# H3 convolution and MLP on one core: copies shared by ScalarE and VectorE get PSUM tiles of their own, two blocks and one output tile go in halves

## Chip, cores and metric

The kernel runs on 1 core of one Trainium2 chip. The metric is device time in microseconds (us). In this text PE is TensorE, PEld its weight loads, ACT is ScalarE, DVE is VectorE, POOL is GpSimd and SP is SyncE; all times are us unless marked otherwise.

## The reference

One layer of an H3 block on 2048 tokens with 512 channels, in bf16, followed by an MLP with 1376 hidden units. The long convolution is computed there with Fourier transforms of length 4096 over the tokens.

```python
def _A_ref(q, k, v, shift_k, ssm_k, ssm_D):
    ...
    for t in range(ks):                                   # ks = 4
        k_shift = k_shift + k_pad[:, t:t + S, :] * shift_k[:, ks - 1 - t][None, None, :]
    kv = k_shift * v
    L = 2 * S
    ...
    kv_f = rfft2(kv_pad[:, None, :, :], axes=(1, 2))      # over 4096 tokens, half of them zero
    kf_f = rfft2(kf_pad[:, None, :], axes=(1, 2))         # the filter ssm_k
    y_f = kv_f * kf_f
    y = irfft2(y_f, s=(1, L), axes=(1, 2)).astype(bf16)[:, 0, :S, :]
    y = y + kv * ssm_D[None, None, :]
    return q * y

x = A_q
h = x + _A_ref(_layernorm(x), A_k, A_v, A_shift_k, A_ssm_k, A_ssm_D)
h2 = h + relu(_layernorm(h) @ B_w1) @ B_w2
return h2
```

## The kernel before

The Fourier transforms are matmuls in two stages each way. The order of instructions on every engine is the order of the source (a manual schedule); the framework places the semaphore waits and gives out buffers.

- **PSUM.** Until inverse stage 1 is over, every PSUM tile comes from one pool, `psF`, of four buffers of two banks each (`bank2`: 128 x 2 x 512 floats). A new tile takes the buffer that the fourth tile before it had, and its first writer waits until that tile's readers are done.
- **Transposition, `to_rows` (lines 271 to 284).** It runs twice: for the filter `sk` (line 311, into `kfl`) and for the product `vT` (line 387, into `xfl`). PE transposes 32 pieces in four groups h = 0 to 3 of eight (line 276). A group fills one PSUM tile `pst` and is copied out into every 32nd column range of the destination: h = 0 and 2 by ACT (line 281), h = 1 by DVE (line 283), and h = 3 by both, four pieces each.
- **Stage 1 (`stage1`, lines 286 to 309).** Sixteen pairs of matmuls (line 294) fill two PSUM tiles. For the filter the two tiles are each read by both engines (DVE line 306, ACT line 309); for the product ACT reads one and DVE the other (lines 267 and 269 through `copy`). Between the filter's groups PE computes the four taps of the short convolution (`taps`, line 333), whose result DVE multiplies with v (line 337). ACT computes sines for the tables of later stages in between.
- **Stage 2 and product (lines 418 to 455).** PE at lines 425 and 435, ACT at 415, DVE at 442, and POOL builds tables at 380.
- **Inverse stage 1 (`inv1`, lines 550 to 562).** Sixteen blocks b. A block has four groups i of three matmuls (line 541) into one PSUM tile `psi`; then one engine copies it out in two pieces, into the two halves of `ax` (one of them lies in the tile `BX`). Blocks 6, 8, 10, 12 and 14 are copied by DVE, block 15 by both engines, two groups each, the others by ACT. Behind the copies of blocks 8 to 11 ACT computes a sine table each (line 262), DVE computes layer norm statistics behind block 0 and normalises behind block 3, and SP loads x behind block 11.
- **Inverse stage 2 and MLP (lines 626 to 712).** For each of four quarters q: `inv2` (line 634), `gate` (DVE, lines 620 and 621), `mlp1` (PE line 646, ReLU on ACT line 648) and `mlp2`. In `mlp2` an output tile of 128 tokens x 512 channels is 11 matmuls (line 659), one DVE pass that scales and adds the residual (line 662), and one store on ACT's queue (line 665). The output buffers `ob` are three, used in turn.

The first matmul of inverse stage 2 needs all 128 columns of `ax`, so it needs the copies of all sixteen blocks. The first of stage 1 needs the whole of `kfl` or `xfl`.

Of the kernel before, what the change touches and what calls it, by code (L numbers as in the profile page):

```python
# [9 lines left out]
ALU = mybir.AluOpType  # L10
BF16 = mybir.dt.bfloat16
F32 = mybir.dt.float32
F32R = mybir.dt.float32r
I32 = mybir.dt.int32
PSUM = bass.MemoryType.PSUM
P = 128
# [40 lines left out]
def kernel(  # L57
# [13 lines left out]
    nc = tc.nc  # L71
    _, S, D = A_q.shape
    DFF = B_w1.shape[1]
    KS = A_shift_k.shape[1]
    assert S == 2048 and D == 512 and KS == 4, "kernel is specialised to S=2048, D=512, ks=4"
    NT = 16
    DC = D // P
    NFC = (DFF + P - 1) // P
    x_d, k_d, v_d, out_d = A_q[0], A_k[0], A_v[0], out[0]
# [70 lines left out]
    def bank2(name):  # L150
        return psum.tile([P, 2, 512], F32, tag="ps", name=name)[:]
# [23 lines left out]
    identw = early.tile([P, P], F32, name="identw")  # L175
# [81 lines left out]
    def ec_wrap(q):  # L257
        nc.vector.tensor_single_scalar(out=ecw[q], in_=ecw[q], scalar=8191, op=ALU.bitwise_and)  # L258

    def ec_sins(q, rs=range(DC)):  # L260
        for r in rs:
            nc.scalar.activation(out=ecore[q][:, :, :, r, :], in_=ecw[q].rearrange("p h (i x) -> p h i x", i=4),  # L262
                                 func=ACT.Sin, scale=esc[:, r:r + 1], bias=ebi[:, r:r + 1])

    def copy(eng, o, i):
        if eng == "A":
            nc.scalar.copy(out=o, in_=i)
        else:
            nc.vector.tensor_copy(out=o, in_=i)

    def to_rows(src, h, fl):

        pst = bank2("pst").rearrange("p b (i c) -> p (b i) c", i=4)
        srcw = src.bitcast(F32).rearrange("p c (a w) -> p (c a) w", w=32)
        for i in range(8):
            nc.tensor.transpose(out=pst[:, i, :], in_=srcw[:, :, 8 * h + i], identity=identw[:])
        o = fl.bitcast(I32)
        for eng, i0, n in {0: (("A", 0, 8),), 1: (("D", 0, 8),), 2: (("A", 0, 8),), 3: (("A", 0, 4), ("D", 4, 4))}[h]:
            oi, pi = o[:, :, 8 * h + i0:8 * h + i0 + n], pst[:, i0:i0 + n, :]
            if eng == "A":  # L280
                nc.scalar.copy(out=oi.bitcast(F32), in_=pi.rearrange("p i c -> p c i"))
            else:
                nc.vector.tensor_single_scalar(out=oi, in_=pi.bitcast(I32).rearrange("p i c -> p c i"),
                                               scalar=0, op=ALU.bitwise_or)

    def stage1(fl, B, gb, dmul=None):
# [24 lines left out]
    for h in range(4):  # L311
        to_rows(sk, h, kfl)
# [74 lines left out]
    for h in range(4):  # L387
        to_rows(vT, h, xfl[:])
# [86 lines left out]
    xh = [None] * 4  # L475

    def load_x(q):
        for a, src in enumerate(_tokens(x_d, 4 * q, 4)):
            nc.sync.dma_start(out=xh[q][32 * a:32 * a + 32].rearrange("p t d -> p (t d)"), in_=src)
# [8 lines left out]
    rstd2 = late.tile([P, NT, 1], F32, name="rstd2")  # L488
# [24 lines left out]
    def ln1_stats(q):  # L513
        stats(xh[q], mv1, rstd1, q)

    def ln1_norm(q, src=None):

        src = xh[q] if src is None else src
        for i in range(4):
            t = 4 * q + i  # L520
            nc.vector.tensor_scalar(out=src[:, i, :], in0=src[:, i, :], scalar1=mv1[:, t, 0:1],
                                    scalar2=rstd1[:, t, :], op0=ALU.subtract, op1=ALU.mult)
        rows_T(qT[q], src)

    def center(n):
        fs = slice(n * FS, (n + 1) * FS)
        nc.vector.tensor_tensor(out=w1[:, :, fs], in0=w1[:, :, fs],
                                in1=cen[n].unsqueeze(1).to_broadcast([P, DC, FS]), op=ALU.subtract)
# [3 lines left out]

    blocks = {}

    def inv1_mm(b, i, parts):
        g = 4 * b + i
        o = blocks[b][:, i].rearrange("p d a n -> p (d a n)")
        for part in parts:
            src = BX[:, 0] if part == 0 else BK[:, part - 1]
            rhs = inv3[:].rearrange("p d a n -> p (d a n)") if part == 0 else inv12[:, 4 - 2 * part:8 - 2 * part, :].rearrange("p a n -> p (a n)")  # L540
            nc.tensor.matmul(out=o, lhsT=src[:, g // 2, :, g % 2::2].rearrange("p c r -> p (c r)"), rhs=rhs,  # L541
                             start=(part == 0), stop=(part == 2), skip_group_check=True)

    def inv1_begin(b):

        blocks[b] = bank2("psi").rearrange("p b (i d a n) -> p (b i) d a n", i=2, d=2, a=2)
        for i in (0, 2):
            inv1_mm(b, i, (0,))

    def inv1(b, eng):  # L550
        if b in blocks:
            for i in range(4):
                inv1_mm(b, i, (0, 1, 2) if i % 2 else (1, 2))
        else:
            blocks[b] = bank2("psi").rearrange("p b (i d a n) -> p (b i) d a n", i=2, d=2, a=2)
            for i in range(4):
                inv1_mm(b, i, (0, 1, 2))
        ps = blocks[b]
        for e, i0, n in ((eng, 0, 4),) if len(eng) == 1 else ((eng[0], 0, 2), (eng[1], 2, 2)):
            for rho in range(2):  # L560
                copy(e, ax[rho][:, :, :, 8 * b + 2 * i0:8 * b + 2 * i0 + 2 * n],
                     ps[:, i0:i0 + n].rearrange("p i d a n -> p a n (i d)")[:, rho].rearrange("p (n m) c -> p n m c", m=2))

    lift(0)
    later = qT[0].rearrange("p i r t -> p (i r t)").bitcast(F32)[:, 0:2 * FS].rearrange("p (n f) -> p n f", n=2)
# [6 lines left out]
    ecw[1] = xr1.rearrange("p i d -> p (i d)").bitcast(I32).rearrange("p (h x) -> p h x", h=2)  # L572
    ec_turns(1)
    for b in range(16):
        inv1(b, "AD" if b == 15 else "D" if b in (6, 8, 10, 12, 14) else "A")
        if b == 0:
            for n in range(4):
                center(n)
            ec_wrap(1)
            ln1_stats(0)  # L580
        if b == 3:
            ln1_norm(0)
        if b in (8, 9, 10, 11):
            ec_sins(1, (b - 8,))
        if b == 11:
            load_x(1)
# [4 lines left out]
    def room(n, pat, **kw):  # L591

        top[0] += n
        assert top[0] <= 32768
        return M[:, top[0] - n:top[0]].rearrange(pat, **kw)

    w2 = room(NFC * 512, "p (c d) -> p c d", c=NFC)
# [54 lines left out]
    def mlp2(sc, hook=None):  # L652
        h1T = h1s[sc]
        for i in range(4):
            t = 4 * sc + i
            ps2 = psm.tile([P, D], F32, tag="ps", name="ps2m")
            for fc in range(NFC):
                ksz = min(P, DFF - fc * P)
                nc.tensor.matmul(out=ps2[:], lhsT=h1T[:ksz, fc, i * P:(i + 1) * P], rhs=w2[:ksz, fc, :],  # L659
                                 start=(fc == 0), stop=(fc == NFC - 1))  # L660
            o = ob[t % 3]
            nc.vector.scalar_tensor_tensor(out=o[:], in0=ps2[:], scalar=rstd2[:, t, :], in1=xh[sc][:, i, :],  # L662
                                           op0=ALU.mult, op1=ALU.add)
            dst = bass.AP(tensor=out_d.tensor, offset=out_d.offset + t * D, ap=[[16 * D, 4], [64 * D, 32], [1, D]])
            nc.scalar.dma_start(out=dst, in_=o)
            if hook is not None:
                hook(i)

# [8 lines left out]
    psm = pl.push("psM", bufs=4, space=PSUM)  # L677
# [11 lines left out]
    def next_norm(q):  # L689
# [7 lines left out]
        return hook  # L697

    mlp2(0, next_norm(2))
    inv2(2, psz)  # L700
    mlp1(1, lambda fc: ec_sins(3, (fc // 2,)) if fc in (1, 3, 5, 7) else None)
    stats(xh[1], mv2, rstd2, 1)
    gate(2)
    mlp2(1, next_norm(3))
    inv2(3, psz)
    mlp1(2)
    stats(xh[2], mv2, rstd2, 2)
    gate(3)
    mlp2(2)
    mlp1(3)  # L710
    stats(xh[3], mv2, rstd2, 3)
# [32 lines left out]
```

## Time and profile before

| what | value |
|---|---|
| runs before | 214.94, 214.96, 216.5; median 214.96 |
| the profiled execution's own time | 214.74 |
| its span, first to last instruction | 213.0 |
| mean granted clock of PE | 0.994 |
| first transposition (line 276) | 9.49 to 13.33 |
| taps and stage 1 of the filter | 14.75 to 36.9 |
| second transposition | 36.91 to 40.73 |
| stage 1 of the product | 42.15 to 51.5 |
| stage 2 and product | 51.56 to 91 |
| inverse stage 1 (line 541) | 90.8 to 114.5 |
| inverse stage 2, gate, MLP | 116.11 to 207.75 |
| last store: issue, end of the span | 208.56, 213.0 |

The profile's rows in order of time read: start, duration, engine, line, operation, output<-input, partitions x elements and type, count; in square brackets how long the engine stood idle before, and what ended that idle time. A row for several instructions spans all of them. "Matmul" rows have ends that are modelled, so the distance between starts tells PE's pace better than their length. The profiled time is a little longer than the span, since the span counts from the first to the last instruction.

### The profile page before, as it was taken

The numbers are of one execution on the slowest core, as the hardware profiler recorded it, in microseconds if no ns is written. First come the engines' busy times: TensorE is split into PE (matmuls) and PEld (weight loads), VectorE is DVE, ScalarE is ACT, GpSimd is POOL, SyncE is SP. The second block draws the span as 40 slices with busy tenths as digits, with TensorE's granted clock in tenths as the row PEclk, the third lists the DMA queues.
The fourth block names the chain that finished last, engine by engine and source line by source line (L and its number), as shares of the span: only waits on it lengthen the run. The fifth ranks groups of instructions, "written<-read, shape, count | busy, mean of one in ns | idle before, by whom it ended". The sixth has DMA issues, their size and how long they took to land. (4 is left out here: it accounts for less than half of the span.)

```text
span 213.0 us, 4286 instructions
## 1 busy us (share of the span) xinstructions
PE 200.3 (94%) x1715; PEld 137.1 (64%) x1724; DVE 141.2 (66%) x243; ACT 115.7 (54%) x186; POOL 70.3 (33%) x119
## 2 busy tenths in 40 slices
PE   7779999999999999999997999999999999999990
PEld 2465555887888888789996954457444844444440
DVE  5978987599678887898743487897078742260121
ACT  3987776687777677657592039501970065026200
POOL 7954703995555893030103022420102110002000
PEclk9999999999999999999999999999999999999997
DMA  5999970001600000037315997999818715110011
GB/s 155 340 219 171 197 118 2 3 5 15 252 3 0 3 0 3 0 99 102 67 32 143 267 210 142 174 170 142 110 33 101 141 24 102 27 57 14 0 51 47
DMA packets 47686, 19.91 MB, mean 93 GB/s; under 512 B 42706, under 2 KB 46132, under 8 KB 47668
## 3 DMA queue, kind: packets, MB, share of 16 engines
q1 hardware_dynamic: 44144, 16.15, 41.1%
q10 hardware_dynamic: 3524, 3.51, 5.6%
q8 instruction: 13, 0.21, 0.5%
q14 instruction: 5, 0.04, 0.1%
HBM read 7.02 MB, written 2.10 MB: 43 GB/s over the span
## 5 line engine op out<-in xcount | busy, mean ns | idle before, releaser
L648 ACT ACTIVATE M<-ps1m 128x512 bf16<-128x512 f32 (+1 forms) x44 | 25.0, 601 | 49.9 <-PE ps1m L646 39.5
L659 PE MATMUL ps2m<-M 128*128 128x512 bf16 (+1 forms) x172 | 38.5, 379 | 0.2
L659 PEld LDWEIGHTS <-M 128*128 128x128 bf16 (+1 forms) x176 | 17.1, 98 | 20.9 <-ACT M L648 0.4
L646 PEld LDWEIGHTS <-w 128*128 128x128 bf16 (+1 forms) x176 | 17.4, 100 | 20.4 <-issue 0.7
L380 POOL TENSOR_TENSOR smc<-st 64x256 fp32r<-64x256 f32 x32 | 22.7, 729 | 11.1 <-PE us L435 10.2
L662 DVE SCALAR_TENSOR_TENSOR M<-ps2m,rstd,M 128x512 bf16<-128x512 f32 x12 | 9.0, 748 | 25.3 <-PE ps2m L659 16.8
L503 POOL TENSOR_SCALAR rstd<-mv 128x4 f32<-128x4 f32 x8 | 2.2, 276 | 70.9 <-DVE mv L501 70.9
L541 PE MATMUL psi<-inv,BK 128*128 128x256 f32 x128 | 22.7, 283 | 0.0
L442 DVE TENSOR_TENSOR BK<-u,ktu 128x512 fp32r<-128x512 f32 x32 | 20.4, 680 | 0.0
L541 PEld LDWEIGHTS psi<-inv,BK 128*128 128x128 f32 x128 | 19.9, 195 | 0.0
L646 PE MATMUL ps1m<-xT,w 128*128 128x512 bf16 (+1 forms) x88 | 19.6, 379 | 0.2 <-ACT M L648 0.2
L646 PE MATMUL ps1m<-M,w 128*128 128x512 bf16 (+1 forms) x88 | 19.3, 379 | 0.0
L541 PE MATMUL psi<-inv,BX 128*128 128x256 f32 x64 | 18.0, 286 | 0.1
L415 ACT COPY ktu<-u 128x512 f32<-128x512 f32 x32 | 17.2, 589 | 1.5
L442 DVE TENSOR_TENSOR BX<-us,kts 128x512 fp32r<-128x512 f32 x16 | 11.1, 691 | 8.4 <-PE u L425 6.7
L415 ACT COPY kts<-us 128x512 f32<-128x512 f32 x16 | 9.4, 587 | 9.5 <-PE us L435 9.5
L425 PE MATMUL u<-BK,st 64*128 64x256 f32 x128 | 14.6, 308 | 0.0
L425 PE MATMUL u<-BX,st 64*128 64x256 f32 x128 | 13.0, 284 | 0.0
L309 ACT CAST BK<-ps 128x512 fp32r<-128x512 f32 x16 | 9.4, 585 | 6.5 <-PE ps L294 3.9
L541 PEld LDWEIGHTS psi<-inv,BX 128*128 128x128 f32 x64 | 12.3, 195 | 0.6 <-DVE BK L442 0.6
L499 DVE BATCH_NORM_STATS2 st<-M 128x6 f32<-128x512 bf16 x20 | 12.3, 677 | 0.0
L435 PE MATMUL us<-BK,smc 128*128 128x256 f32 x64 | 12.0, 310 | 0.0
(127 smaller groups left out, 399.3 us busy)
## 6 DMA issues: line engine op xcount, KB each, us to landing
E<-in_A_ssm_k_dram SPq DMA_DIRECT2D x1, 2048.0 KB
out_dram<-M ACTq DMA_DIRECT2D x16, 128.0 KB
w<-in_B_w_dram SPq DMA_DIRECT2D x1, 1376.0 KB
M<-in_B_w_dram ACTq DMA_DIRECT2D x1, 1280.0 KB
M<-in_A_q_dram SPq DMA_DIRECT2D x8, 128.0 KB
xh<-in_A_q_dram SPq DMA_DIRECT2D x4, 128.0 KB
xr<-in_A_q_dram SPq DMA_DIRECT2D x4, 128.0 KB
M<-in_B_w_dram ACTq DMA_DIRECT2D x1, 96.0 KB
```

The costliest lines, as they stand in the source:

```text
L309: nc.scalar.copy(out=o[1 - rp][:, 1], in_=pv[1 - rp][:, 1])
L380: nc.gpsimd.tensor_tensor(out=smc[pq, c % 4, i, :, 64 * dp:64 * dp + 64], in0=st[pq, ks, 64:128].bitcast(F32), in1=st[pq, ks, 0:64].bitcas ...
L415: nc.scalar.copy(out=kt[:], in_=ps)
L425: nc.tensor.matmul(out=ps[:, dp, 256 * x:256 * x + 256], lhsT=t[pq], rhs=cols((BK, BX)[x], pq, k1, i), start=(i == 0), stop=(i == 1), tile ...
L435: nc.tensor.matmul(out=ps[:, k % 2, 256 * x:256 * x + 256], lhsT=smc[:, k // 4 % 4, i, k % 4, :], rhs=cols((BK, BX)[x], slice(0, P), k, i) ...
L442: nc.vector.tensor_tensor(out=o, in0=ps[:, :, 256:512].rearrange("p b (g x) -> p b g x", x=8), in1=kt[:].rearrange("p b (g x) -> p b g x", ...
L499: nc.vector.bn_stats(out=st[:, i, :], in_=src[:, i, :])
L541: nc.tensor.matmul(out=o, lhsT=src[:, g // 2, :, g % 2::2].rearrange("p c r -> p (c r)"), rhs=rhs, start=(part == 0), stop=(part == 2), sk ...
L646: nc.tensor.matmul(out=ps1[:fsz, :].rearrange("p (i t) -> p i t", i=4), lhsT=w1[:, c, fc * P:fc * P + fsz], rhs=hT[sc][:, :, c, :], start= ...
L648: nc.scalar.activation(out=h1T[:fsz, fc, :], in_=ps1[:fsz, :], func=ACT.Relu)
L659: nc.tensor.matmul(out=ps2[:], lhsT=h1T[:ksz, fc, i * P:(i + 1) * P], rhs=w2[:ksz, fc, :], start=(fc == 0), stop=(fc == NFC - 1))
L662: nc.vector.scalar_tensor_tensor(out=o[:], in0=ps2[:], scalar=rstd2[:, t, :], in1=xh[sc][:, i, :], op0=ALU.mult, op1=ALU.add)
```

## The change

- In `to_rows` each copy gets a PSUM tile of its own. For h = 0, 1 and 2 nothing differs. For h = 3 the four transposes of ACT's half go into one tile and the four of DVE's half into another; each tile takes a whole buffer of the pool and uses half of it.
- In `inv1` the same is done for blocks that are shared: two groups into a tile, its copies, then two groups into a second tile, its copies. Blocks 14 and 15 are now shared; blocks 7, 9, 11 and 13 go to DVE (before: 6, 8, 10, 12 and 14), the others to ACT.
- In `mlp2` the last of the 16 output tiles is computed, passed through DVE and stored in two halves of 256 channels: 22 matmuls of 256 columns instead of 11 of 512, two DVE passes, two stores of 128 rows of 512 bytes.

```diff
     def to_rows(src, h, fl):
-        pst = bank2("pst").rearrange("p b (i c) -> p (b i) c", i=4)
...
-        for i in range(8):
-            nc.tensor.transpose(out=pst[:, i, :], in_=srcw[:, :, 8 * h + i], identity=identw[:])
...
+        for eng, i0, n in {1: (("D", 0, 8),), 3: (("A", 0, 4), ("D", 4, 4))}.get(h, (("A", 0, 8),)):
+            pst = bank2("pst").rearrange("p b (i c) -> p (b i) c", i=4)[:, 0:n]
+            for i in range(n):
+                nc.tensor.transpose(out=pst[:, i, :], in_=srcw[:, :, 8 * h + i0 + i], identity=identw[:])
...
     def inv1(b, eng):
...
-        ps = blocks[b]
-        for e, i0, n in ((eng, 0, 4),) if len(eng) == 1 else ((eng[0], 0, 2), (eng[1], 2, 2)):
+        n = 4 // len(eng)
+        for i0, e in zip((0, 2), eng):
+            if b not in blocks or i0:
+                blocks[b] = bank2("psi").rearrange("p b (i d a n) -> p (b i) d a n", i=2, d=2, a=2)
+                todo = [(i, (0, 1, 2)) for i in range(n)]
...
+            for i, parts in todo:
+                inv1_mm(b, i, parts, i0)
             for rho in range(2):
                 copy(e, ax[rho][:, :, :, 8 * b + 2 * i0:8 * b + 2 * i0 + 2 * n],
...
-        inv1(b, "AD" if b == 15 else "D" if b in (6, 8, 10, 12, 14) else "A")
+        inv1(b, "AD" if b > 13 else "D" if b in (7, 9, 11, 13) else "A")
...
             o = ob[t % 3]
-            nc.vector.scalar_tensor_tensor(out=o[:], in0=ps2[:], ...)
-            dst = bass.AP(tensor=out_d.tensor, offset=out_d.offset + t * D, ap=[[16 * D, 4], [64 * D, 32], [1, D]])
-            nc.scalar.dma_start(out=dst, in_=o)
+            w = D // 2 if t == NT - 1 else D
+            for d0 in range(0, D, w):
+                ps2 = psm.tile([P, D], F32, tag="ps", name="ps2m")[:, 0:w]
+                for fc in range(NFC):
+                    ksz = min(P, DFF - fc * P)
+                    nc.tensor.matmul(out=ps2, lhsT=h1T[:ksz, fc, i * P:(i + 1) * P], rhs=w2[:ksz, fc, d0:d0 + w],
+                                     start=(fc == 0), stop=(fc == NFC - 1))
+                nc.vector.scalar_tensor_tensor(out=o[:, d0:d0 + w], in0=ps2, ...)
+                dst = bass.AP(tensor=out_d.tensor, offset=out_d.offset + t * D + d0, ap=[[16 * D, 4], [64 * D, 32], [1, w]])
+                nc.scalar.dma_start(out=dst, in_=o[:, d0:d0 + w])
```

More of the change, by code (lines that the diff above doesn't have):

```diff
@@ L271, in to_rows @@
     def to_rows(src, h, fl):
-        pst = bank2("pst").rearrange("p b (i c) -> p (b i) c", i=4)
         srcw = src.bitcast(F32).rearrange("p c (a w) -> p (c a) w", w=32)
-        for i in range(8):
-            nc.tensor.transpose(out=pst[:, i, :], in_=srcw[:, :, 8 * h + i], identity=identw[:])
         o = fl.bitcast(I32)
-        for eng, i0, n in {0: (("A", 0, 8),), 1: (("D", 0, 8),), 2: (("A", 0, 8),), 3: (("A", 0, 4), ("D", 4, 4))}[h]:
-            oi, pi = o[:, :, 8 * h + i0:8 * h + i0 + n], pst[:, i0:i0 + n, :]
+        for eng, i0, n in {1: (("D", 0, 8),), 3: (("A", 0, 4), ("D", 4, 4))}.get(h, (("A", 0, 8),)):
+            pst = bank2("pst").rearrange("p b (i c) -> p (b i) c", i=4)[:, 0:n]
+            for i in range(n):
+                nc.tensor.transpose(out=pst[:, i, :], in_=srcw[:, :, 8 * h + i0 + i], identity=identw[:])
+            oi = o[:, :, 8 * h + i0:8 * h + i0 + n]
             if eng == "A":
-                nc.scalar.copy(out=oi.bitcast(F32), in_=pi.rearrange("p i c -> p c i"))
+                nc.scalar.copy(out=oi.bitcast(F32), in_=pst.rearrange("p i c -> p c i"))
             else:
-                nc.vector.tensor_single_scalar(out=oi, in_=pi.bitcast(I32).rearrange("p i c -> p c i"),
+                nc.vector.tensor_single_scalar(out=oi, in_=pst.bitcast(I32).rearrange("p i c -> p c i"),
                                                scalar=0, op=ALU.bitwise_or)
@@ L533, with inv1_mm @@
     blocks = {}
-    def inv1_mm(b, i, parts):
-        g = 4 * b + i
+    def inv1_mm(b, i, parts, i0=0):
+        g = 4 * b + i0 + i
         o = blocks[b][:, i].rearrange("p d a n -> p (d a n)")
@@ L550, in inv1 @@
     def inv1(b, eng):
[L551 to L557, printed above, removed]
-        ps = blocks[b]
-        for e, i0, n in ((eng, 0, 4),) if len(eng) == 1 else ((eng[0], 0, 2), (eng[1], 2, 2)):
+        n = 4 // len(eng)
[3 more added lines that the diff above has]
+                todo = [(i, (0, 1, 2)) for i in range(n)]
+            else:
+                todo = [(i, (0, 1, 2) if i % 2 else (1, 2)) for i in range(n)]
+            for i, parts in todo:
+                inv1_mm(b, i, parts, i0)
             for rho in range(2):
                 copy(e, ax[rho][:, :, :, 8 * b + 2 * i0:8 * b + 2 * i0 + 2 * n],
-                     ps[:, i0:i0 + n].rearrange("p i d a n -> p a n (i d)")[:, rho].rearrange("p (n m) c -> p n m c", m=2))
+                     blocks[b][:, 0:n].rearrange("p i d a n -> p a n (i d)")[:, rho].rearrange("p (n m) c -> p n m c", m=2))
     lift(0)
@@ L655, in mlp2 @@
             t = 4 * sc + i
[L656 to L660, printed above, removed]
-            o = ob[t % 3]
-            nc.vector.scalar_tensor_tensor(out=o[:], in0=ps2[:], scalar=rstd2[:, t, :], in1=xh[sc][:, i, :],
-                                           op0=ALU.mult, op1=ALU.add)
-            dst = bass.AP(tensor=out_d.tensor, offset=out_d.offset + t * D, ap=[[16 * D, 4], [64 * D, 32], [1, D]])
-            nc.scalar.dma_start(out=dst, in_=o)
+            o = ob[t % 3]
+            w = D // 2 if t == NT - 1 else D
[5 more added lines that the diff above has]
+                                     start=(fc == 0), stop=(fc == NFC - 1))
+                nc.vector.scalar_tensor_tensor(out=o[:, d0:d0 + w], in0=ps2, scalar=rstd2[:, t, :], in1=xh[sc][:, i, d0:d0 + w],
+                                               op0=ALU.mult, op1=ALU.add)
+                dst = bass.AP(tensor=out_d.tensor, offset=out_d.offset + t * D + d0, ap=[[16 * D, 4], [64 * D, 32], [1, w]])
+                nc.scalar.dma_start(out=dst, in_=o[:, d0:d0 + w])
             if hook is not None:
```

## The prediction

> **What bounds the kernel now.** I read the page's busy times first, then the busy time by stage, then the order of instructions around each edited place, and last what moves after the last matmul. TensorE (PE) is at work for 94% of the span, so a change pays only where PE stands still, or behind PE's last matmul.
>
> ```profile
> PE 200.3 (94%) x1715; PEld 137.1 (64%) x1724; DVE 141.2 (66%) x243; ACT 115.7 (54%) x186; POOL 70.3 (33%) x119
> ```
>
> The edits touch four places. In the first transposition PE waits for the last copy, in the order of time:
>
> ```profile
> 11.57 1.23 DVE L283 TENSOR_SCALAR E<-pst 128x1024 int32<-128x1024 int32 x1 [0.37 <-PE pst L276]
> 12.47 1.50 ACT L281 COPY E<-pst 128x1024 f32<-128x1024 f32 x2 [0.69 <-PE pst L276]
> 14.00 0.69 DVE L283 TENSOR_SCALAR E<-pst 128x512 int32<-128x512 int32 x1 [1.21 <-ACT E L281]
> ...
> 14.75 0.23 PE L294 MATMUL ps<-f_hi,E 64*128 64x128 bf16 x2 [1.42 <-DVE E L283]
> ```
>
> VectorE (DVE) is free from 12.80, the last transpose ends at 9.49 + 3.84 = 13.33, yet DVE starts its half at 14.00, when ScalarE (ACT) has done the other half of the same tile. The same wait of 1.21 stands in the second transposition:
>
> ```profile
> 39.87 1.50 ACT L281 COPY xfl<-pst 128x1024 f32<-128x1024 f32 x2 [0.78 <-PE pst L276]
> ...
> 41.41 0.69 DVE L283 TENSOR_SCALAR xfl<-pst 128x512 int32<-128x512 int32 x1 [1.21 <-ACT xfl L281]
> 41.80 0.59 ACT L309 CAST BK<-ps 128x512 fp32r<-128x512 f32 x1 [0.43 <-PE ps L294]
> 42.01 1.28 DVE L306 TENSOR_TENSOR BK<-ps,dmask 128x512 fp32r<-128x512 f32 x2
> ...
> 43.34 1.23 DVE L269 CAST BX<-ps 128x1024 fp32r<-128x1024 f32 x1
> 43.38 1.01 ACT L267 CAST BX<-ps 128x1024 fp32r<-128x1024 f32 x1
> ```
>
> The last two rows say that it is the shared PSUM tile that makes the wait: there the engines copy from tiles of their own into interleaved columns of one output, and they run side by side. At the end of inverse stage 1 the wait is on the path, for PE stands idle until DVE is done:
>
> ```profile
> 114.52 0.37 ACT L267 CAST BX<-psi 128x256 fp32r<-128x256 f32 x1 [1.80 <-PE psi L541]
> ...
> 114.79 0.38 ACT L267 CAST ax<-psi 128x256 fp32r<-128x256 f32 x1
> ...
> 115.20 0.42 DVE L269 CAST BX<-psi 128x256 fp32r<-128x256 f32 x1 [0.83 <-ACT ax L267]
> ...
> 115.54 0.41 DVE L269 CAST ax<-psi 128x256 fp32r<-128x256 f32 x1
> 116.11 0.36 PE L634 MATMUL pz<-core,BX 128*128 128x256 f32 x1 [1.39 <-DVE ax L269]
> ```
>
> And behind PE's last matmul stand one VectorE pass and one store; the windows (PE, PEld, DVE, ACT, POOL busy, clock, DMA share, GB/s) show bytes until about 211.45, then nothing:
>
> ```profile
> 207.78 0.75 DVE L662 SCALAR_TENSOR_TENSOR M<-ps2m,rstd,M 128x512 bf16<-128x512 f32 x1 [1.63 <-PE ps2m L659]
> ```
> ```profile
> 207.25:209.25 2.00, 0.49 (x3) 0.00 (x0) 0.75 (x1) 0.00 (x0) 0.00 (x0) 1.00 0.22 66
> 209.25:211.50 2.25, 0.00 (x0) 0.00 (x0) 0.00 (x0) 0.00 (x0) 0.00 (x0) 0.74 0.20 58
> 211.50:213.00 1.50, 0.00 (x0) 0.00 (x0) 0.00 (x0) 0.00 (x0) 0.00 (x0) 0.50 0.00 0
> ```
>
> **First transposition: 0.59 us saved.** No instruction is added, only one more of the four PSUM buffers is taken. Its transposes reuse the buffer of h=0, copied by 10.79 + 0.99 = 11.78, while they start at about 12.7 (28 transposes at 0.115, which is 3.84 less the 0.275 of one, over 31): no stall. DVE's start follows the last transpose as 11.57 follows the sixteenth, by 0.08: 13.41, and 0.69 later it ends at 14.10. ACT's half ends at 12.47 + 1.50 = 13.97. PE's stage 1 starts 0.06 behind, at 14.16 and not 14.75. What follows until the second transposition is paced by PE: its stage 1 starts at 20.61, 23.44, 26.28 and 29.12, every 2.83, and DVE in each round waits 0.33 to 0.53 for PE's taps. The loads do not shift, but their SyncE (SP) rows end at 28.64 and DMA is silent from 31.0, while DVE uses the last of them at 33.79. So the whole 0.59 is carried on. DVE's wrap at 14.61 moves to 14.02, behind the GpSimd (POOL) row that feeds it and ends at 13.78. If a load or that POOL row were the hidden bound, the saving would be 0: bounds 0 and 0.65.
>
> **Second transposition: nothing.** DVE's half can start at 40.81 instead of 41.41 (0.08 behind the last transpose at 40.73). But PE works on stage 1 of the last filter group in between (40.66 to 41.73), and does not need this copy. The extra buffer shifts who waits for whom: that stage's second PSUM tile stood four behind h=1 (free at 40.20), and now four behind h=2, whose ACT copy ends at 39.87 + 1.01 = 40.88. PE waits there about 0.22, so L309 and L306 start at about 42.02, against 41.80 and 42.01. DVE's L306 pair, then L269, follow back to back, and DVE sets the pace of the next stage (10.65 of 10.90 busy from 42.1 to 53). It starts where it did. I take 0; bounds: 0.10 lost, 0.21 won if the buffer is free sooner.
>
> **End of inverse stage 1: 0.68 saved.** DVE's half of block 15 waits only for its own matmuls, and they end at 114.09 + 0.40 = 114.49, as ACT's first copy showed at 114.52. DVE's two copies then run from 114.52 to 115.27, as they now run from 115.20 to 115.95, and PE starts inverse stage 2 at 115.43. ACT's half is ready at about 113.8 and done at 114.5. Block 14 in halves is done on DVE at 113.85. PE keeps its 192 matmuls, at 0.12 each, and hardly waited there (23.41 busy of 23.5).
>
> The engines of blocks 6 to 14 are swapped by one. ACT now has blocks 8, 10 and 12 with the four sines between them: 104.47 + 0.94 (pair of copies) + 2 x 1.14 (sines) + 0.94 + 2.28 gives 110.91, and block 12 is done at 111.95. Behind ACT's sines waits SP's load of x (now at 111.41): it goes 0.4 earlier. POOL's tables and the load of w2 on ACT's queue wait for PE's last matmul, which stays. DVE's block 13 is done at 112.94. Block 15's two tiles need the buffers of blocks 12 and 13 at 113.05 and 113.77: 1.1 and 0.8 to spare, and that spare is what hides this edit. Late next, after 115.43, is PE's own inverse stage 2, then the gate, the statistics and ACT's sines down to 132.8; the chain that ended last runs through them, all started by it, and PE is dense behind. Bounds 0.55 and 0.70.
>
> **Last output tile: 0.65 saved.** PE gets 22 matmuls of 256 columns for 11 of 512. The nearest rows are L634's, 256 columns with a weight load each, at 0.117 apart: 22 x 0.117 = 2.57 against 11 x 0.216 = 2.38, so 0.19 lost (bounds 0 and 0.27, by L541's 0.12). VectorE's pass shrinks as its 256- and 512-wide casts do, 0.42 to 0.69: 0.75 to 0.46, 0.29 won. The group starts at 205.37; the halves end on PE at 206.66 and 207.94, on DVE at 207.15 and 208.43, and the stores are issued at 207.18 and 208.46 (0.55 each on ACT's queue, with nothing else behind). The store alone thus starts 0.10 sooner. Bytes begin 1.05 behind an issue (208.56 to 209.6). The store before moves bytes from 207.25 to 209.1, at 0.28 of the DMA engines, so the first half queues behind it. A 128 KB store takes 1.75, 1.33 at the 98 GB/s of its later part. A half takes 0.67 if bytes count, 1.35 if its 128 rows count as they do at 1 KB; I take 0.85, nearer to the bytes, for the rate is steady. The second half's bytes could begin at 209.51 but find the first's until 209.95, which hides both PE's 0.19 and VectorE's 0.29; without that cover they are a net gain of 0.10. Halves end at 209.95 and 210.80, against 211.45: 0.65 saved; with rows alone 211.80, 0.35 lost; with bytes alone 210.5, 0.95 saved. What follows the bytes (1.55) stays. The first half's pass needs its output buffer back from the fourth store from the end, bytes until 204.5 and 1.55 more: 206.05, and it starts at 206.69, so no wait is added there.
>
> A rule speaks against this edit: the Trainium skill, "DMA: Bandwidth & Descriptors", section Bandwidth, calls transfers under 64 KB dominated by descriptors, and lists 0.95 us for 64 KB. By it the halves would end at 211.0 and the whole saving would be 0.2 smaller. No row here has a transfer of 64 KB in such rows.
>
> **The sum.** 0.59 + 0 + 0.68 + 0.65 = 1.92. The profiled execution took 214.74 around its span of 213.0, so it would take 212.82; the median of the runs is 0.22 higher, 213.04. I forecast 213.0.
>
> **Rivals.** (a) Rows and not bytes set the halves' store: 0.59 + 0.68 - 0.35 = 0.92 saved, 214.0. For it: the share of 0.28 says few engines carry a store. Against: the steady 98 GB/s. (b) The early saving is swallowed before inverse stage 1, because a load or POOL sets the start of a later step: 1.33 saved, 213.6. Against: PE is the releaser in every round. (c) The upper ends: the second transposition wins 0.21, the stores 0.95: 2.43 saved, 212.5. (d) The copies still wait on each other, because their outputs interleave: only the stores gain, 214.3. Against: the rows at 43.34 and 43.38. (e) The slower side: ACT's copies of block 12 come so late, behind four sines and blocks 8 and 10, that block 15's first tile finds no free buffer. It decides when they end after 113.05, and the kernel gets slower when they end 1.92 later still, after 114.97; if each of the four sines cost one more of its 1.14, they would end at 116.5, 3.46 late, and the time would be 216.5. Against: the 111.95 above.
>
> **How the numbers follow.** Forecast 0.48, (a) 0.13, (b) 0.09, (c) 0.22, (d) 0.05, (e) 0.03. About 1% is what a measurement of this kernel can tell from no change, here 2.15 saved, below 212.81. The forecast's own range is 212.6 to 213.5, and some 0.11 of its 0.48 lies below that line; with (c) that gives 0.33 for faster. Slower by over 1% is (e), 0.03. The rest, 0.64, is within 1%. The range 212.2 to 214.1 takes in (a), (b) and (c) and leaves out (d), (e) and the far ends.
>
> **What would show it.** Right: no wait of DVE L283 for ACT; stage 1 at about 14.16; the step from L276's last transpose to L269's first copy in the second transposition unchanged, with PE waiting about 0.2 inside it; PE's gap ahead of L634 about 0.7 and not 1.4; no wait of PE for ACT or DVE between blocks 12 and 15; bytes ending some 3 us behind PE's last matmul, against 3.7 now. Wrong: the start of stage 1 earlier but the start of inverse stage 1 not; or the last half's bytes taking over 1.2.

## The result and the profile after

| | before | after |
|---|---|---|
| median of the runs | 214.95 (4 runs) | 212.98 (4 runs) |
| profiled execution: own time, span | 214.74, 212.96 | 213.07, 211.25 |
| mean granted clock of PE | 0.994 | 1.000 |

By the medians 1.97 us are saved, by the two profiled spans 1.71; the ratio of the mean times is 0.9893, with a 95% interval of 0.9852 to 0.9933. Single executions of several of the kernels took some 1.5 more at a lower mean clock (two later ones of the kernel before: 216.35 and 216.41 at 0.986); the last section shows one from inside. In the listing after, lines below `to_rows` have moved: the transposes stand at 278, the matmuls of `mlp2` at 662, its DVE pass at 664.

The page of the changed kernel, part 1, answers to the first line shown of before:

```profile
PE 201.9 (96%) x1735; PEld 138.5 (66%) x1735; DVE 141.4 (67%) x244; ACT 116.1 (55%) x188; POOL 70.4 (33%) x119
```

PE's share went up because the span shrank around nearly the same work; that its busy time reads 1.6 more is mostly a gap in the record of before, which has 1715 matmuls for 1724 weight loads. The timeline of the first transposition after:

```profile
11.64 1.23 DVE L283 TENSOR_SCALAR E<-pst 128x1024 int32<-128x1024 int32 x1 [0.41 <-PE pst L278]
...
12.92 0.52 PEld L278 LDWEIGHTS pst<-identw,E 128*128 128x128 f32 x4 [0.16 <-DVE E L283]
13.67 0.69 DVE L283 TENSOR_SCALAR E<-pst 128x512 int32<-128x512 int32 x1 [0.81 <-PE pst L278]
...
14.28 1.22 DVE L220 TENSOR_SCALAR G<-G 128x2048 int32<-128x2048 int32 x1
...
14.51 0.23 PE L294 MATMUL ps<-f_hi,E 64*128 64x128 bf16 x2 [0.88 <-DVE E L283]
```

DVE's second row now waits for PE and no longer for ACT: the wait of 1.21 is gone. But the weight loads' row ahead of it is new. PE's last four transposes wait for DVE's copy of h = 1, which ends at 11.64 + 1.23 = 12.87. The row of line 220 is VectorE's "wrap" of the prediction; it stood at 14.61 before. The second transposition, in two pieces of its timeline, of which the first ends with DVE's half and the second is PE's stage 1 of the last filter group:

```profile
36.58 3.83 PE L278 MATMUL pst<-identw,E 128*128 128x128 f32 x32 [0.43 <-PE ps L294]
...
40.44 0.69 DVE L283 TENSOR_SCALAR xfl<-pst 128x512 int32<-128x512 int32 x1 [0.57 <-PE pst L278]
```
```profile
40.34 0.48 PE L294 MATMUL ps<-f_hi,E 64*128 64x128 bf16 x2
...
40.62 0.26 PE L294 MATMUL ps<-f_lo,E 64*128 64x128 bf16 x2
40.68 0.25 PE L294 MATMUL ps<-f_hi,E 64*128 64x128 bf16 x2
```

Here the 32 transposes run through (3.83, as before), and the stall sits in the stage 1 behind them: from 40.34 to the next start it is 0.28, and from there to the one after 0.06, so some 0.22 is lost. The timeline of the end of inverse stage 1:

```profile
113.77 0.40 PE L541 MATMUL psi<-inv,BK 128*128 128x256 f32 x2
...
114.21 0.42 DVE L269 CAST BX<-psi 128x256 fp32r<-128x256 f32 x1 [0.68 <-PE psi L541]
...
115.11 0.36 PE L634 MATMUL pz<-core,BX 128*128 128x256 f32 x1 [0.49 <-DVE ax L269]
```

DVE starts 0.04 behind the last matmul (113.77 + 0.40 = 114.17) and not 0.71 behind it. Last, the end, as the timeline and as windows (busy PE, PEld, DVE, ACT, POOL, clock, DMA share, GB/s):

```profile
204.48 0.75 DVE L664 SCALAR_TENSOR_TENSOR M<-ps2m,rstd,M 128x512 bf16<-128x512 f32 x1 [1.63 <-PE ps2m L662]
...
205.69 0.48 DVE L664 SCALAR_TENSOR_TENSOR M<-ps2m,rstd,M 128x256 bf16<-128x256 f32 x1 [0.46 <-PE ps2m L662]
206.89 0.48 DVE L664 SCALAR_TENSOR_TENSOR M<-ps2m,rstd,M 128x256 bf16<-128x256 f32 x1 [0.72 <-PE ps2m L662]
```
```profile
207.25:209.25 2.00, 0.00 (x0) 0.00 (x0) 0.12 (x1) 0.00 (x0) 0.00 (x0) 1.00 0.28 90
209.25:209.75 0.50, 0.00 (x0) 0.00 (x0) 0.00 (x0) 0.00 (x0) 0.00 (x0) 1.00 0.28 85
209.75:211.20 1.45, 0.00 (x0) 0.00 (x0) 0.00 (x0) 0.00 (x0) 0.00 (x0) 1.00 0.00 0
```

The last bytes have moved by 209.78 (before: by 211.54, 0.09 later than the prediction read from its windows), and until then the store before and the two halves follow each other without a gap, at the same DMA share of 0.28 as a whole store had.

**Where the time went.** The table gives how far after is ahead of before at each place, counted from the start of the first transposition (9.49 before, 9.56 after).

| place | before | after | ahead | step |
|---|---|---|---|---|
| first matmul of stage 1 | 14.75 | 14.51 | 0.31 | 0.31 |
| second round of the taps (line 333) | 18.77 | 18.44 | 0.40 | 0.09 |
| second transposition | 36.91 | 36.58 | 0.40 | 0 |
| stage 2 of the product (line 435, second group) | 53.05 | 52.71 | 0.41 | 0.01 |
| last matmul of inverse stage 1, end | 114.49 | 114.17 | 0.39 | -0.02 |
| inverse stage 2 | 116.11 | 115.11 | 1.07 | 0.68 |
| DVE pass of the last but one output tile | 205.40 | 204.48 | 0.99 | -0.08 |
| last bytes | 211.54 | 209.78 | 1.83 | 0.84 |
| end of the span | 212.96 | 211.25 | 1.78 | -0.05 |

Less the 0.07 of the later start, that is the 1.71 between the spans.

### The profile page after: what moved, and what is told of

It reads as the page before. It is cut to its first block, busy times and chain, and to the rows that moved or that the text cites. A ratio compares the mean times of both kernels' runs of the same rounds, so it can differ in the third digit from the quotient of the medians.

```text
span 211.2 us, 4330 instructions
## 1 busy us (share of the span) xinstructions
PE 201.9 (96%) x1735; PEld 138.5 (66%) x1735; DVE 141.4 (67%) x244; ACT 116.1 (55%) x188; POOL 70.4 (33%) x119
## 4 chain that ended last, share of the span: by engine, by line
PE 84%; DVE 5%; DMA 4%; ACT 4%; issue 1%; SPq 0%; DVEq 0%
PE ps2m L662 18%; PE ps1m L646 14%; PE psi L541 11%; PE u L425 9%; PE us L435 9%; PE ps L294 8%; PE pkv L333 7%; PE pz L634 5%; DMA E<-in_A_ssm_k_dram 4%; PE pst L278 3%; ACT BX L262 2%; DVE st L499 1%; ACT M L648 1%; DVE qT L620 1%; ACT xfl L281 0%
## 5 line engine op out<-in xcount | busy, mean ns | idle before, releaser
L662 PE MATMUL ps2m<-M 128*128 128x512 bf16 (+3 forms) x187 | 38.8, 366 | 0.0
L662 PEld LDWEIGHTS <-M 128*128 128x128 bf16 (+1 forms) x187 | 18.2, 98 | 20.0 <-ACT M L648 0.4
L664 DVE SCALAR_TENSOR_TENSOR M<-ps2m,rstd,M 128x512 bf16<-128x512 f32 (+1 forms) x13 | 9.2, 708 | 24.3 <-PE ps2m L662 15.7
```

What stands on the lines that cost most here:

```text
L662: nc.tensor.matmul(out=ps2, lhsT=h1T[:ksz, fc, i * P:(i + 1) * P], rhs=w2[:ksz, fc, d0:d0 + w], start=(fc == 0), stop=(fc == NFC - 1))
```

## The experiments

In every kernel of this section the transposing transfers (of k, v, the normalised x and h) are plain transfers of the same bytes, so those values stay untransposed. The first two runs are the two kernels with that one replacement; the others are compared with them.

**The two kernels as the base.** The edit, in one of its places:

```diff
-        nc.sync.dma_start_transpose(out=vT[:, :, CH * c:CH * c + CH], in_=v_d[CH * c:CH * c + CH, :])
+        nc.sync.dma_start(out=vT[:, :, CH * c:CH * c + CH], in_=v_d[CH * c:CH * c + CH, :].rearrange("(p r) t -> p r t", r=DC))
```

> The kernel before, with its 20 transposing transfers (k and v at the start, the normalised x, the gate's results) as plain copies of the same bytes to the same places, so that these values stay untransposed. It is the base for the runs with single parts. PE sets the pace from the first transposition on, and the transposing transfers were waited for only in the gates, by DVE, with PE 9 us behind: so the time stays within 0.5 of 214.95. Rival: the load of the filter shares the DMA engines with the transposing loads, and lands sooner by some tenths; then all of it shifts, 213.5 to 214.5. PE's gap ahead of inverse stage 2 and the wait of the second copy stay as they were: 1.6 and 1.2.

> The changed kernel with the same 20 transfers as plain copies. If the transfers play no part in the change, the difference to the base with plain copies is that of the originals, 1.97 by the medians (1.7 to 1.8 by the spans). A difference under 1.4 or over 2.4 would say that the transposing transfers have a share in it.

The kernel before took 214.59 in this form, 0.9993 (0.9984 to 1.0003) of its original; the changed one 212.81, 0.991 (0.9893 to 0.9926). The difference is 1.78. The waits are the same: first transposition to stage 1 5.26 and 4.94, last matmul of inverse stage 1 to stage 2 some 1.6 and 0.93. So these kernels stand for the originals, within some 0.2. One source of that is seen in their traces: the first transposition starts when the filter's load lands, between 9.22 and 9.61 from run to run.

**One part at a time.** Each kernel is the plain one before with one part of the change: `to_rows` alone, `inv1` and its engines alone, `mlp2` alone.

```diff
p2_rows_alone
-        pst = bank2("pst").rearrange("p b (i c) -> p (b i) c", i=4)
+        for eng, i0, n in {1: (("D", 0, 8),), 3: (("A", 0, 4), ("D", 4, 4))}.get(h, (("A", 0, 8),)):
+            pst = bank2("pst").rearrange("p b (i c) -> p (b i) c", i=4)[:, 0:n]
p3_inverse_alone
-        inv1(b, "AD" if b == 15 else "D" if b in (6, 8, 10, 12, 14) else "A")
+        inv1(b, "AD" if b > 13 else "D" if b in (7, 9, 11, 13) else "A")
p4_tail_alone
+            w = D // 2 if t == NT - 1 else D
+            for d0 in range(0, D, w):
```

> Base with plain copies, and only the transposition's part of the change. Theory from the trace after: the first transposition gives 0.3 (stage 1 starts 0.31 sooner behind the first transpose), the second nothing, and that is carried to the end: 0.3 below the base. Rival, the record's step: 0.59 is there to be had, and something later in the changed kernel ate half of it: then this part alone gives 0.55 to 0.6. In the trace, theory: one wait of PE's transposes of h = 3 for DVE's copy of h = 1, about 0.15.

> Base with plain copies, and only inverse stage 1's part, with blocks 14 and 15 in halves and the engines swapped. Theory: PE's gap ahead of inverse stage 2 shrinks from 1.62 to 0.94, 0.68 below the base. Rival: 0.1 of it is given back in inverse stage 2, as the trace after hints (1.00 ahead at its start, 0.91 at the gate): 0.58 below the base.

> Base with plain copies, and only the last output tile in two halves. The base stood at 214.59 with the unchanged kernel at 214.78. Theory: the three parts add up, and 1.78 less 0.46 less 0.63 leaves 0.69 for this one; the trace after says 0.78 by the bytes' end. So 0.65 to 0.8 below the base. Rival: rows and not bytes set the store, 0.1 below to 0.3 above the base; the trace after already speaks against it.

| part | median | ratio to before (95%) | against the plain kernel before |
|---|---|---|---|
| `to_rows` | 214.13 | 0.9971 (0.9959 to 0.9983) | 0.46 saved |
| `inv1` | 213.96 | 0.9965 (0.9952 to 0.9978) | 0.63 saved |
| `mlp2` | 213.69 | 0.9949 (0.9934 to 0.9964) | 0.90 saved |

The sum is 1.99, against 1.78 for all three together. The shifting start is in these medians. Counted in the traces from the start of the first transposition to the end of the span, the three parts save 0.42, 0.59 and 0.81, in sum 1.82, and all three together 1.85: the parts add up.

With `to_rows` alone the timeline shows the stall in the same place, and stage 1 starts 4.93 behind the first transpose:

```profile
12.60 0.53 PEld L278 LDWEIGHTS pst<-identw,E 128*128 128x128 f32 x4 [0.16 <-DVE E L283]
...
14.19 0.23 PE L294 MATMUL ps<-f_hi,E 64*128 64x128 bf16 x2 [0.88 <-DVE E L283]
```

At stage 2's line 435 this kernel is 0.42 ahead of the original before (43.14 against 43.56 from the first transpose), which is what the whole change shows there; the early saving does reach the end (0.46 by the medians, 0.42 by the traces). It lies between the theory's 0.3 and the rival's 0.55: stage 1 is 0.33 ahead, as the theory has it, and some 0.08 more come until the second round of the taps. With `inv1` alone the gap ahead of inverse stage 2 shrinks by 0.68, but 0.05 of it is given back before the last output tiles; the 0.63 lies between theory and rival too, and why the 0.05 is lost stays open. With `mlp2` alone the last but one tile's pass stands at 205.25 in both kernels, the last bytes at 210.55 instead of 211.40, and the span is 212.0 instead of 212.8: 0.80 by the trace, of which nothing can come from anywhere else. The medians say 0.90, above the 0.65 to 0.8 that was expected.

**Block 15 alone.** `inv1` of the change with the engines of before, so that block 14 stays whole and on DVE:

```diff
-        inv1(b, "AD" if b > 13 else "D" if b in (7, 9, 11, 13) else "A")
+        inv1(b, "AD" if b == 15 else "D" if b in (6, 8, 10, 12, 14) else "A")
```

> Base with plain copies, inverse stage 1 with block 15 in halves and tiles of its own, but block 14 whole and the engines of blocks 6 to 14 as before (DVE has 6, 8, 10, 12, 14). Theory: block 14 in halves and the swap do nothing for the time; DVE ends its copies of block 14 just ahead of its half of block 15, so this gives what the whole part gave, 0.63 below the base (0.55 to 0.7). Rival: DVE is late with block 14 and the last half waits for it: 0.2 to 0.4 below the base.

It took 213.90 (0.9963, 0.995 to 0.9976), 0.69 saved: as much as with block 14 in halves and the engines swapped. The timeline shows why:

```profile
113.50 0.68 DVE L269 CAST ax<-psi 128x512 fp32r<-128x512 f32 x1
...
114.33 0.42 DVE L269 CAST BX<-psi 128x256 fp32r<-128x256 f32 x1
```

DVE has done block 14 at 113.50 + 0.68 = 114.18, and its half of block 15 begins at 114.33. The second of the "last two blocks" and the swap cost nothing and bring nothing.

**VectorE's half first.** If the stall of PE is the price of h = 3 having two tiles, the order of the two halves should decide whom it falls on:

```diff
-        for eng, i0, n in {1: (("D", 0, 8),), 3: (("A", 0, 4), ("D", 4, 4))}.get(h, (("A", 0, 8),)):
+        for eng, i0, n in {1: (("D", 0, 8),), 3: (("D", 0, 4), ("A", 4, 4))}.get(h, (("A", 0, 8),)):
```

> The changed kernel with plain copies (212.81), where in h = 3 of the transpositions DVE takes the first four pieces and ACT the last four. Theory: half of the first transposition's expected saving was lost because the second tile of h = 3 got the buffer that DVE's long copy of h = 1 gives back late, so PE stalled and DVE's half, the last of all, came later. With DVE first, its tile has a buffer that is free, the stall of about 0.15 falls on ACT's half, whose engine is busy with h = 2 anyway: stage 1 starts 0.1 to 0.15 sooner, 212.68. Rival: it is the second wait on two engines ahead of stage 1, not the stall, that costs: no change, 212.8; or the stall only moves to ACT and the end is the same.

212.70 (0.9902, 0.9887 to 0.9916), 0.11 better than the plain changed kernel.

```profile
11.33 2.04 DVE L283 TENSOR_SCALAR E<-pst 128x1024 int32<-128x1024 int32 x2 [0.50 <-PE pst L278]
...
12.61 0.53 PEld L278 LDWEIGHTS pst<-identw,E 128*128 128x128 f32 x4 [0.16 <-DVE E L283]
...
13.78 1.23 DVE L220 TENSOR_SCALAR G<-G 128x2048 int32<-128x2048 int32 x1 [0.41 <-POOL G L238]
...
14.00 0.23 PE L294 MATMUL ps<-f_hi,E 64*128 64x128 bf16 x2 [0.68 <-ACT E L281]
```

The stall stays (0.16, and behind the same DVE copy), but now ACT's half, the later of the two, ends at 13.95, and PE follows 0.05 behind it, where it followed 0.15 behind DVE's half. Stage 1 starts 4.73 behind the first transpose, 0.53 less than before and 0.21 less than in the changed kernel, so the rival, by which the end stays the same, is out. DVE is done so early that its wrap now waits 0.41 for the POOL row that feeds it: the hidden bound that the prediction named is reached here.

**Block 15 in pieces of two groups, one and one.** What is left of the gap ahead of inverse stage 2 is a DVE half of 256 columns; smaller last pieces on both engines should shorten it.

```diff
-        inv1(b, "AD" if b > 13 else "D" if b in (7, 9, 11, 13) else "A")
+        inv1(b, (("A", 2), ("D", 1), ("A", 1)) if b == 15 else ...)     # pieces of n groups, each in a PSUM tile of its own
```

> The changed kernel with plain copies (212.81), where block 15 goes in three tiles: two groups on ACT, one on DVE, the last one on ACT. Theory: PE's gap ahead of inverse stage 2 is now made of the two copies of 128x256 behind the last matmul; two of 128x128 on ACT take about 0.43 instead of 0.75 (0.59, 0.37 and then about 0.26 for 512, 256 and 128 columns), so 0.3 less: 212.5. Rival: a third tile makes PE wait for a buffer in block 15, or ACT is not done with the first two groups: 0.1 less or none.

212.45 (0.9893, 0.9876 to 0.9909), 0.36 better. From the stand-in matmuls behind the last block (`psz`) to inverse stage 2 it is 113.70 to 114.41, 0.71 instead of 1.09:

```profile
114.06 0.28 ACT L267 CAST ax<-psi 128x128 fp32r<-128x128 f32 x1
...
114.41 0.36 PE L633 MATMUL pz<-core,BX 128*128 128x256 f32 x1 [0.32 <-ACT ax L267]
```

**Spreading the last stores.** A store of this kernel keeps the DMA engines busy to 0.28. The Trainium skill, "DMA: Bandwidth & Descriptors", section "Why a DMA increments its semaphore by 16 and not by 1", says that the slowest dimension of each side decides how many of the 16 engines take part; the output's is 4, which by this rule makes an estimate of 4 of 16. The row agrees so far (0.28). Four transfers of 32 rows, on the queues of SP and ACT, should then use more of them:

```diff
-                nc.scalar.dma_start(out=dst, in_=o[:, d0:d0 + w])
+                for a in range(4):          # last tile only
+                    dst = bass.AP(tensor=out_d.tensor, offset=out_d.offset + (16 * a + t) * D + d0, ap=[[64 * D, 32], [1, w]])
+                    (nc.scalar if a % 2 else nc.sync).dma_start(out=dst, in_=o[32 * a:32 * a + 32, d0:d0 + w])
```

> The changed kernel with plain copies (212.81), where each half of the last output tile is stored in four transfers of 32 rows, in turn on SP's and ACT's queues. Theory: a store with all 128 rows moves at 0.28 of the DMA engines, and its halves queue behind each other and behind the store of the tile before, bytes without a gap for 3.4. Transfers of 32 rows, as the loads of x are, spread over more engines; then the end follows the last issue: two issues of 0.5 behind DVE's last pass, 1.05 to the first byte, 0.2 of bytes, so bytes end some 0.6 sooner: 212.2. Rival: the rate belongs to the queue that hands out rows, not to the engines; two queues then halve the 1.5 at best, and the extra issues eat that: 212.6 to 212.9.

212.61 (0.9911, 0.9888 to 0.9934), 0.20 better, a third of what the theory says. The time lies in the rival's range, but not for the rival's reason, a rate that belongs to the queue. A window of 0.5 shows that more engines do take part, and the queue rows show what it costs:

```profile
207.50:208.00 0.50, 0.00 (x0) 0.00 (x0) 0.00 (x0) 0.00 (x0) 0.00 (x0) 1.00 0.59 161
```
```profile
205.86 2.71 SPq L670 DMA_DIRECT2D out_dram<-M  x4
205.87 2.05 ACTq L670 DMA_DIRECT2D out_dram<-M  x4
```

The share is 0.59, twice that of one store. But the second half's transfers can only be issued behind DVE's pass, which ends at 207.03. ACT's queue issues its two by 207.92, SP's its two by 208.57, and the bytes of that last one move from 209.1 to 209.3.

**All three, and two variants of the store.** VectorE's half first and block 15 in 2, 1 and 1 in one kernel, with both halves spread (p9), with the change's two half-stores (p10), and with the second half alone spread (p11).

> The changed kernel with plain copies (212.81) and the three edits together: DVE's half first in h = 3 (0.11 less alone), block 15 in tiles of two, one and one groups (0.36 less alone), the last tile's stores in 32 rows on two queues. Theory: they lie one behind the other on the same path and add up: 212.34 less what the stores alone give, 211.7 if that is 0.6. Rival: gains overlap (the stores' end is set by the tile before, whose bytes shift too, but the issue does not): 212.0 or more.

> The changed kernel with the plain input copies (212.81) and two further edits: VectorE's half of h = 3 first, and block 15 copied in pieces of two groups, one and one. The stores of the last tile are the change's two half-stores. If the gains of the single runs add up (0.11 and 0.36): 212.34, and the part of the spread stores inside the run of all three (212.02) is then 0.32, more than their 0.20 alone. Rival: the two edits overlap, because a part of the early time is given back before the last tile: 212.22 or less is then excluded, and the time is 212.45 as with block 15 alone.

> The same kernel, but the second half of the last tile alone is stored in four transfers of 32 rows on the queues of SP and ACT; the first half goes in one store on ACT's queue. If the queues' issue time sets the end of the spread stores (each queue's two issues of the second half wait for its two of the first), the last issue comes some 0.1 sooner than with both halves spread, and the time is 211.9. If the bytes set it (the first half at a quarter of the DMA engines runs until some 208.3 and the second finds those engines busy): 212.1 to 212.3.

| kernel | median | ratio (95%) | range of the runs at the usual clock |
|---|---|---|---|
| p9, both halves spread | 212.02 | 0.9875 (0.9857 to 0.9892) | 211.97 to 212.27 |
| p10, half-stores | 212.17 | 0.9879 (0.9838 to 0.992) | 212.14 to 212.18 |
| p11, second half spread | 212.35 | 0.9897 (0.986 to 0.9934) | 211.95 to 212.35 |

The two edits on PE's path add up: counted in the traces from the first transposition to the last but one output tile, VectorE's half first brings 0.13, block 15 in pieces 0.34, and both in p9 0.50. By the medians p10 is 0.64 better than the plain changed kernel, where 0.11 + 0.36 = 0.47 was expected, with an interval too wide to tell the two apart; the rival 212.45 falls. From that tile to the end of the span the kernels with two half-stores take 6.75 to 6.77, p6 6.57 and p9 6.56, so both halves spread bring 0.18 to 0.19, in p9 as alone. This is why p9's 212.02 lies in its rival's "212.0 or more": it is the spread that brings less than the 0.6 hoped for, not the other gains that overlap. In p11 the same stretch is 6.61: 0.14, which the medians do not show. That p11 brings less than p9 is the surprise, because its bytes are done earliest (windows of 0.5, last two columns DMA share and GB/s; 0.58 and 152 in the window ahead of these):

```profile
208.00:208.50 0.50, 0.00 (x0) 0.00 (x0) 0.00 (x0) 0.00 (x0) 0.00 (x0) 1.00 0.32 83
208.50:209.00 0.50, 0.00 (x0) 0.00 (x0) 0.00 (x0) 0.00 (x0) 0.00 (x0) 1.00 0.00 0
```

The last byte moves at 208.44 and the span ends at 210.25: 1.81 behind it, where two stores leave 1.47 (after) and both spread halves 1.41 (p9: 208.77 and 210.18). So in p11 the last byte no longer sets the end. What does is in SP's waits, of which the last ones are those at the end of the program (us in total, how often, the longest). First p11, then p9:

```profile
SPq L745 <- DMA out_dram<-M: 1.8, 2, 1.6
```
```profile
SPq L745 <- DMA out_dram<-M: 1.0, 1, 1.0
```

SP stands there until every store has signalled that it is done. In the trace each store signals 16 times. Of p11's four spread transfers twelve signals each have come by 208.60. The last four of a transfer come together, and one transfer follows the other: at 208.74, 208.92, 209.10 and 209.28, behind the signals of the first half's store at 208.56. SP goes on after 209.28, which is 0.84 behind the last byte. In p9 eight transfers end in the same ladder, 0.18 apart, the last one at 209.16, 0.39 behind the last byte; in the changed kernel the last signal comes 0.37 behind it. So the first theory of p11 falls: its issues do end sooner, but the time is not 211.9. The second one has the place nearly right: something is still late behind the first half's store, but it is the signals and not the bytes. Its 212.1 to 212.3 holds the profiled run (212.23), while the median of 212.35 lies just above. That the four late signals of a transfer belong to the DMA engines that carry the first half is argued and not shown, and why each signal takes 0.18 stays open.

## Why the prediction was right, and where not

The total was right: 1.92 saved was forecast, the medians say 1.97, the spans 1.71. The split was not: the first transposition gave 0.28 less than its term and the last tile 0.19 more, and smaller steps in between cancelled too. That the total is so close is luck. The mechanism was right: copies that no longer wait for each other at the places named, and bytes that end sooner.

- **First transposition, 0.59 forecast, 0.31 measured.** The wait of DVE for ACT went, as said. The step that failed is "Its transposes reuse the buffer of h=0 ...: no stall". The last tile got the buffer of h = 1, and PE had to wait for DVE's copy of it until 12.87. The 32 transposes took 4.07 instead of 3.84, which is 0.23; PE started 0.15 behind DVE's end (14.36 to 14.51), where the sum took 0.06, which is 0.09 and stays open; and DVE followed the last transpose in 0.04 and not 0.08 (13.63 to 13.67). Together that is the 0.28 that is missing. With the halves in the other order, 0.53 of the 0.59 is there. My rule "a new tile takes the buffer that the fourth tile before it had" was read from the pool's size, and the first transposition breaks it: in the compiled program its five tiles begin in PSUM banks 6, 2, 4, 0 and 2, so the last has the buffer of h = 1. Block 15's second tile breaks it too: it has the buffer of block 14's first half, free at 112.70, and not that of block 13, and nothing waits for it either way. In the second transposition the rule holds.
- **What followed it.** "So the whole 0.59 is carried on": what there was of it (0.31) was, and another 0.09 came until the second round of taps. So "paced by PE" does not hold up to there: that round starts 4.16 behind DVE's wrap in both kernels (18.77 - 14.61 and 18.44 - 14.28; 4.16 to 4.18 in thirteen of the profiles), but 4.02 and 3.93 behind stage 1. The wrap came 0.40 sooner, and so did the round. Nor does DVE wait for PE's taps "in each round": ahead of its rows of line 337 at 17.69 and 26.49 the trace before has no wait. Rival (b), the early saving swallowed, is out: `to_rows` alone gains 0.46. But POOL as the hidden bound is near: with VectorE's half first, the wrap waits 0.41 for it.
- **Second transposition, 0 forecast, 0.01 measured.** The stall foreseen in the last filter group is there, at the size foreseen (0.22), and the waits of 1.21 are gone without a gain, since other work sets the pace of the stage behind.
- **End of inverse stage 1, 0.68 forecast, 0.68 measured** (1.62 to 0.94 from the last matmul to inverse stage 2). The cover named there held: ACT's copies of block 12 are done at 111.06 + 0.61 = 111.67, no row of line 541 shows PE waiting, and rival (e) did not come near. What the prediction did not see is that block 15 in halves does it all alone (0.69), and that 0.08 is given back until the last but one output tile; why stays open.
- **Last output tile, 0.65 forecast, 0.84 measured (0.79 at the end of the span).** PE lost next to nothing: a group of 11 matmuls of 256 columns took 1.205 (the distance between the DVE passes), so 2.41 for both against 2.38, 0.03 and not 0.19: the row of another matmul form (0.117) was too slow for this one (0.110). DVE's half pass took 0.48 (0.46 forecast). All this is hidden, as said: the transfers follow without a gap, 208.26 to 209.02 to 209.78. So the term was mis-sized in the bytes. A half-store took 0.76 (0.85 forecast, bounds 0.67 and 1.35), which makes 0.18 for both; the store before ended 0.08 later than forecast; and 0.09 is the end of the bytes before, 211.54 where the prediction read 211.45. Bytes count and not rows. Rival (a) is out. The Trainium skill, "DMA: Bandwidth & Descriptors", section "Bandwidth", has its 0.95 for 64 KB from loads into SBUF that GpSimd issued; for this store on ACT's queue the row decides, 0.76.
- **Rivals (c) and (d).** (c)'s whole gain at the last tile (0.95) was about as much too high as the forecast's 0.65 was too low, its gain in the second transposition is not there. (d), copies that still wait because their outputs interleave, is out: no copy waits for another one in any of the four places.

The best version in these runs is p9 or, without the spread stores, p10: 212.02 and 212.17 against 212.81 for the plain changed kernel. The combination with the transposing transfers was not run.

## What to carry to other kernels

When two engines share the reading of one tile, look for the row of the second engine whose wait is ended by the first; a tile of its own removes that wait, but the time is won only where the second engine's end releases the engine on the path, and it can matter which engine stands last: with ACT's copy at the end, one variant was 0.11 better. Each further tile also takes a buffer, and the trace, not the pool's size, says whose reader has to be done with it. A last output in halves pays while its bytes are the end; cut finer, the issues on the queues take over, and then the signals of the single transfers, which came later than their bytes.

## What was not expected of the hardware

- Once the last stores were spread, an end of the bytes at 208.44 instead of 208.77 did not bring the end of the span forward (210.25 and 210.18). The last signals of the spread transfers came one after the other, 0.18 apart, and the last of them 0.84 (p11) and 0.39 (p9) behind the last byte.
- The issue of a transfer of 16 KB is not in proportion cheaper than that of a whole store: 0.55 for 128 KB on ACT's queue, 0.44 for one of 16 KB (two in 0.87 in p11), and on SP's queue two took 0.80 in p11, but some 1.5 behind two others (207.03 to 208.57 with both halves spread).
- In the profile of p10 the clock drops in the middle of dense work. In windows of 0.5 (busy PE, PEld, DVE, ACT, POOL, then the granted clock):

```profile
10.00:10.50 0.50, 0.50 (x7) 0.50 (x6) 0.50 (x1) 0.10 (x1) 0.50 (x1) 1.00 1.08 363
...
11.00:11.50 0.50, 0.50 (x5) 0.50 (x4) 0.00 (x0) 0.42 (x1) 0.50 (x4) 0.50 1.17 415
...
13.50:14.00 0.50, 0.50 (x4) 0.50 (x3) 0.00 (x0) 0.50 (x1) 0.31 (x1) 0.50 1.20 395
```

  For 3.41 us in the middle of the transposes (10.68 to 14.09) the clock is granted at half, and the 32 transposes take 5.43 instead of 4.06. In this trace PE had stood idle for 1.83 ahead of the transposes, longer than in any other of the profiles (0.20 to 1.71); one trace does not show that this is the cause. The Trainium skill, "TensorE: Matmul & The Clock Gate", part 1, tells of a half-rate state entered after idling; its idle window of some 3.4 us is longer than the idle time here.
